# Gated linear attention and a leaky-ReLU block in one kernel: chunks taken in pairs, two tokens per partition

## The chip, the core and the metric

The kernel runs on one core of one Trainium2 chip. The metric is the device time of one execution in microseconds (us), the median of several runs. The profile is one further execution, and its times count from the span's start.

## The reference

Attention with a decaying state, then a two-layer block on its output (batch 4, 8 heads, 768 tokens, head size 48; 3072 tokens of 384 features; hidden size 2048). All inputs are float32.

```python
f = 1 / (1 + exp(-f_logit))
for t in range(768):
    state = f[:, :, t, :, None] * state + outer(k[:, :, t], v[:, :, t])
    y[:, :, t] = q[:, :, t] @ state
x = y.transpose(0, 2, 1, 3).reshape(3072, 384)
h = x @ w_in                      # 384 x 2048
out = maximum(0.01 * h, h) @ w_out  # 2048 x 384
```

## The kernel before

**Units.** A unit is one chunk of 128 tokens of one batch, all heads: 24 units, unit u being chunk u // 4 of batch u % 4, so four neighbouring units are the same chunk of the four batches. Everything that follows attention treats two units (a "pair" m of units 2m and 2m+1) as 256 columns.

**Attention of a unit.** `load_part` loads f, k, q and v on SP's queue, one token per partition: runs of 48 floats, 192 bytes. `gate_exp` and `gate_ln` on ACT give ln(1 + exp(-f)); `gate_pe` sums it over the tokens with a triangular matrix, and with a column of ones gives the chunk's total; `decay_em` and `decay_a` (ACT) are exp of plus and minus that sum, and also the chunk's total decay. `k_scale` and `q_scale` (VectorE or GpSimd) multiply k and q by them and write bf16. `turn_pe` with `turn_k`, `turn_q` (units 4 to 9), or one DMA transpose of two units, `turn2_dma` (units 10 to 23), turn both into kT and qT. `score_pe` multiplies them, `mask` keeps the causal half, `mix_pe` adds the old state's part (qT with `state_b`) and the masked part, `y_out` copies y to bf16, and `x_pe` with `x_out`, or `x2_dma`, turn it into xT. `state_pe`, `state_dve` and `state_pool` carry the state on.

**The block.** For each pair, `up` (eight groups g of 6 matmuls, weights from w_in, 256 columns), `up_act` (ACT, leaky ReLU into gT), then `down` (two halves of 8 matmuls of 384 columns for each unit), `put` into `osb`, and `out_dma`.

**The first four units** (chunk 0 of all batches) run in a special order (functions `q_...`): four tokens per partition, 32 partitions per batch, so runs of 768 bytes, and v is brought into place by the matmuls of `q_pick`. Weights come by GpSimd's queue: `load_w_in` in two halves, `load_w_out` in four quarters.

**Order.** The schedule is manual: after the functions stands a list of some 800 calls, and each engine and queue carries out its own part of it in that order. PE never skips a matmul whose operand is late, and SP's queue holds all loads, turns and stores, one behind the other. All rings (`raws` of 6 units, `kqs` of 4, and so on) are fixed buffers.

Of the kernel before, what the change touches and what calls it, by code (L numbers as in the profile page):

```python
# [15 lines left out]
def kernel(  # L17
# [10 lines left out]
    nc = tc.nc  # L28
# [4 lines left out]
    NCH = S // C  # L33
# [3 lines left out]
    CH = KD // 2  # L37

    units = [(c, b) for c in range(NCH) for b in range(B)]
    NU = len(units)
    NQ = B

    GBUFS = 5
    R_RAW, R_KQS, R_LF, R_EM, R_AEND, R_V, R_KQT, R_WM, R_XN, R_XT = 6, 4, 3, 3, 8, 6, 4, 4, 4, 4
    const = ctx.enter_context(tc.tile_pool(name="const", bufs=1))
    opool = ctx.enter_context(tc.tile_pool(name="opool", bufs=8))
    psum = ctx.enter_context(tc.tile_pool(name="psum", bufs=1, space=bass.MemoryType.PSUM))
    banks = [psum.tile([128, 512], FP32, name=f"ps{i}", tag=f"ps{i}") for i in range(8)]  # L50

    def ring(name, n, shape, dtype):
        return [const.tile(shape, dtype, name=f"{name}{i}", tag=f"{name}{i}") for i in range(n)]

    def bank(i):
        return banks[i][:, :]

    def bank16(i):
        return banks[i][:, :].bitcast(BF16)

    ctx.enter_context(tc.manual_schedule())


    fq = const.tile([128, H, 4, D], FP32, tag="fq")
    kq = const.tile([128, H, 4, D], FP32, tag="kq")
    qq = const.tile([128, H, 4, D], FP32, tag="qq")

    def first_load(eng, name, b, hh=None):
        h = slice(0, H) if hh is None else slice(4 * hh, 4 * hh + 4)
        eng.dma_start(out=fq[32 * b:32 * b + 32, h, :, :].rearrange("p h j d -> p h (j d)"),  # L70
                      in_=f_logit[b, h, 0:C, :].rearrange("h (t j) d -> t h (j d)", j=4))

    def load_all(t, src):
        nc.sync.dma_start(out=t.rearrange("p h j d -> p h (j d)"),  # L74
                          in_=src[:, :, 0:C, :].rearrange("b h (t j) d -> t b h (j d)", j=4))
# [12 lines left out]
    ut = const.tile([128, 128], BF16, tag="ut")
    make_upper_triangular(nc, ut, val=1.0, diag=True)
    us = const.tile([128, 128], BF16, tag="us")  # L90
    make_upper_triangular(nc, us, val=1.0, diag=False)
    ident = const.tile([128, 128], BF16, tag="ident")
    make_identity(nc, ident)
    ones_col = const.tile([128, 1], BF16, tag="ones")
    nc.gpsimd.memset(ones_col, 1.0)

    w_in_b = [const.tile([128, NK, FF // 2], BF16, name=f"w_in{i}", tag=f"w_in{i}") for i in range(2)]
    w_in_p = [t.rearrange("p a (g n i) -> p a g n i", n=128, i=4) for t in w_in_b]
    w_out_b = const.tile([128, NF, KD], BF16, tag="w_out")
# [3 lines left out]
    lfq = [const.tile([128, 4, 4, 64], BF16, name=f"lfq{i}", tag=f"lfq{i}") for i in range(2)]
    khq = [const.tile([128, 4, 4, 64], BF16, name=f"khq{i}", tag=f"khq{i}") for i in range(2)]
    qhq = [const.tile([128, 4, 4, 64], BF16, name=f"qhq{i}", tag=f"qhq{i}") for i in range(2)]
    for t in lfq + khq + qhq:
        nc.vector.memset(t[:, :, :, D:64], 0.0)

    lfs = [const.tile([128, H, 64], BF16, name=f"lf{i}", tag=f"lf{i}") for i in range(R_LF)]
    kqp = ring("kqh", R_KQS // 2, [128, 2, 2, H, 64], BF16)  # L110
    kqs = [kqp[i // 2][:, i % 2] for i in range(R_KQS)]
    khs, qhs = [t[:, 0] for t in kqs], [t[:, 1] for t in kqs]
    state_f = [const.tile([128, P2, D], FP32, name=f"sf{b}", tag=f"sf{b}") for b in range(B)]
    state_b = [const.tile([128, P2, 2 * D], BF16, name=f"sb{b}", tag=f"sb{b}") for b in range(B)]


    block = const.tile([128, 2, 32], BF16, tag="block")
    for b in range(B):
        r = slice(32 * b, 32 * b + 32)
        for i, t in enumerate((ut, us)):  # L120
            nc.vector.tensor_copy(out=block[r, i, :], in_=t[r, r])
    steps = const.tile([128, 4, 32, 4], BF16, tag="steps")
    for i in range(4):
        for t, j0, j1 in ((0, i, 4), (1, 0, i)):
            if j1 > j0:
                nc.vector.tensor_copy(out=steps[:, i, :, j0:j1],
                                      in_=block[:, t, :, None].to_broadcast([128, 32, j1 - j0]))
    for t in lfs:
        nc.vector.memset(t[:, :, D:64], 0.0)
    for t in kqs:  # L130
        nc.vector.memset(t[:, :, :, D:64], 0.0)
    for t in state_b:
        nc.vector.memset(t, 0.0)

# [11 lines left out]


    raws = {name: ring(name, R_RAW, [128, H, D], FP32) for name in ("f_raw", "k_raw", "q_raw", "v_raw")}
    em_ts = ring("em_t", R_EM, [128, H, D], BF16)
    a_ts = ring("a_t", R_EM, [128, H, D], BF16)  # L150
    a_ends = ring("a_end", R_AEND, [128, P2], FP32)
    a_rows = ring("a_row", 2, [128, 2, 64, P2], FP32) if AEND else []
    for t in a_rows:
        nc.gpsimd.memset(t[96:128, :, D:64, :], 1.0)
    v_bs = ring("v_b", R_V, [128, H, D], BF16)
    kqTp = ring("kqT", R_KQT // 2, [128, 2, 2, P2, 128], BF16)
    kqTs = [kqTp[i // 2][:, i % 2] for i in range(R_KQT)]
    turned = {"kT": [t[:, 0] for t in kqTs], "qT": [t[:, 1] for t in kqTs]}
    wms = [ring(f"wm{e}", R_WM, [128, P2, 128], BF16) for e in range(2)]
    xnp = ring("xn", R_XN // 2, [128, 2, KD], BF16)  # L160
    xns = [xnp[i // 2][:, i % 2] for i in range(R_XN)]
    xTs = ring("xT", R_XT, [128, NK, 2, 128], BF16)
    gTs = ring("gT", GBUFS, [128, NF, 2, 128], BF16)
    raw = {}

    def load_part(u, name, src, eng=nc.sync):
        c, b = units[u]
        t = raws[f"{name}_raw"][u % R_RAW]
        eng.dma_start(out=t, in_=src[b, :, c * C:(c + 1) * C, :].rearrange("h t d -> t h d"))  # L169
        raw.setdefault(u, {})[name] = t  # L170

    def load(u):
        for name, src in (("f", f_logit), ("k", k), ("q", q), ("v", v)):
            load_part(u, name, src)

    seen = const.tile([128, 1], FP32, tag="seen")

    def touch(what):
        src = {"f": fq[:, 0, 0, 0:1], "k": kq[:, 0, 0, 0:1], "q": qq[:, 0, 0, 0:1],
               "v": raws["v_raw"][1][:, 0, 0:1], "w": raws["v_raw"][3][:, 0, 0:1]}[what]  # L180
        nc.gpsimd.tensor_copy(out=seen, in_=src)

    def load_w_in(g):
        w = FF // 2
        nc.gpsimd.dma_start(out=w_in_b[g],
                            in_=moe_w_in.rearrange("(a p) n -> p a n", p=128)[:, :, g * w:(g + 1) * w])

    def load_w_out(g):
        w = NF // 4
        nc.gpsimd.dma_start(out=w_out_b[:, g * w:(g + 1) * w, :],  # L190
                            in_=moe_w_out.rearrange("(g p i) n -> p g i n", p=128, i=w)[:, g, :, :])

    st = {u: {} for u in range(NU)}
# [88 lines left out]
    def q_k_mul(hh, pp, bp, bk):  # L282
        q_mul(kTq, emT, hh, pp, bp, bk)
# [1119 lines left out]
```

## Time and profile before

| what | us |
|---|---|
| runs | 182.78, 182.24, 180.99; median 182.24 |
| the profiled execution: its span (no time of its own beside the span is given) | 180.2 |
| PE busy, share of the span | 171.4, 95% |
| ACT, VectorE, GpSimd busy | 124.4, 92.0, 57.9 |
| first matmul of `up` starts | 21.1 |
| units 0 to 3 are mixed, pair 0 and most of pair 1 are up and 20 matmuls of `down` have started | by 34.5 |

The span is the profiler's, from the first to the last instruction; a run is 2.0 us longer than it by the median. PE's busy time counts a matmul from start to its modelled end, and neighbours overlap; a matmul's share of PE's time is therefore read from the distance between starts.

### The profile page before, as it was taken

What the parts mean: (1) busy time and instruction counts of PE and PEld (TensorE: products, weight loads), DVE (VectorE), ACT (ScalarE), POOL (GpSimd) and SP (SyncE); (2) the same over time, 40 slices, a digit from 0 to 9 for tenths busy, and PEclk for the clock granted to TensorE, in tenths of its full rate; (3) what the DMA queues carried; (4) which work ended last, traced back from release to release, by engine and by line L of the source; (5) the groups of instructions that cost most, each with busy time, mean ns of one, the idle gap of its engine ahead of it and who ended that gap; (6) DMA issues with size and microseconds to landing.
All of it is one profiled execution on the core that took longest, in us unless ns stands there. A gap on an engine that the chain in (4) does not pass through costs nothing.

```text
span 180.2 us, 4849 instructions
## 1 busy us (share of the span) xinstructions
PE 171.4 (95%) x1919; PEld 137.8 (76%) x1919; DVE 92.0 (51%) x211; ACT 124.4 (69%) x264; POOL 57.9 (32%) x107
## 2 busy tenths in 40 slices
PE   7689999999999999899999999999999999999992
PEld 5365899677878897597789687789876697798672
DVE  7779860287888735335376186696543266000000
ACT  2779999286887789767488776668795562596331
POOL 7077570023256444700446052634072100000000
PEclk9999999999999999999999999999999999999999
DMA  5999999899997989999699899999999982720112
GB/s 154 312 299 162 197 208 214 156 201 190 155 205 125 215 172 224 165 216 208 147 239 251 181 183 185 209 213 173 203 155 209 224 237 48 60 77 0 44 48 86
DMA packets 109398, 31.31 MB, mean 174 GB/s; under 512 B 100800, under 2 KB 108096, under 8 KB 109376
## 3 DMA queue, kind: packets, MB, share of 16 engines
q1 hardware_dynamic: 107440, 27.47, 79.5%
q0 software_dynamic: 1376, 3.15, 9.5%
q10 hardware_dynamic: 560, 0.39, 0.7%
q8 instruction: 15, 0.25, 0.7%
q14 instruction: 7, 0.06, 0.1%
HBM read 25.17 MB, written 4.72 MB: 166 GB/s over the span
## 4 chain that ended last, share of the span: by engine, by line
PE 58%; SPq 25%; DMA 11%; issue 1%; ACT 1%; DVE 1%; DVEq 0%
SPq L169 24%; PE ps L482 24%; PE ps L502 23%; DMA v_raw<-in_v_dram 6%; DMA f_raw<-in_f_logit_dram 3%; PE ps L420 2%; DMA fq<-in_f_logit_dram 2%; PE ps L441 2%; PE ps L507 1%; PE ps L438 1%; PE ps L348 1%; SPq L74 1%; PE ps L472 1%; PE ps L449 1%; DVE v_b L145 1%
## 5 line engine op out<-in xcount | busy, mean ns | idle before, releaser
L502 PE MATMUL ps<-w_out_b,gT 128*128 128x384 bf16 x368 | 65.9, 326 | 0.0
L487 ACT ACTIVATE gT<-ps 128x512 bf16<-128x512 f32 x88 | 51.5, 602 | 19.1 <-PE ps L482 16.7
L482 PE MATMUL ps<-xT,w_in 128*128 128x256 bf16 x528 | 63.3, 273 | 1.0 <-DVE xT L145 1.0
L482 PEld LDWEIGHTS <-w_in 128*128 128x128 bf16 x528 | 56.4, 114 | 3.0 <-issue 1.2
L502 PEld LDWEIGHTS <-gT 128*128 128x128 bf16 x368 | 34.6, 98 | 19.8
L431 DVE TENSOR_TENSOR wm<-ps,ut 128x512 bf16<-128x512 f32 x40 | 24.9, 683 | 14.5 <-ACT gT L487 4.9
L370 POOL TENSOR_TENSOR kqh<-k_raw,em_t 128x384 bf16<-128x384 f32 x12 | 11.4, 951 | 33.3 <-ACT em_t L355 28.1
L143 ACT COPY osb<-ps 128x384 f32<-128x384 f32 (+1 forms) x22 | 10.2, 465 | 17.0 <-PE ps L502 15.2
L332 POOL CAST sb<-sf 64x192 bf16<-64x192 f32 x40 | 14.5, 363 | 14.9 <-PE ps L438 12.8
L145 DVE CAST v_b<-v_raw 128x384 bf16<-128x384 f32 x14 | 7.1, 505 | 16.0 <-DMA v_raw<-in_v_dram 15.9
L374 DVE TENSOR_TENSOR kqh<-q_raw,a_t 128x384 bf16<-128x384 f32 x13 | 10.0, 770 | 8.0 <-DMA q_raw<-in_q_dram 7.3
L339 ACT ACTIVATE f_raw<-f_raw 128x384 f32<-128x384 f32 x20 | 10.6, 532 | 4.8 <-DMA f_raw<-in_f_logit_dram 4.6
L342 ACT ACTIVATE lf<-f_raw 128x384 bf16<-128x384 f32 x20 | 10.5, 527 | 0.4
L358 ACT ACTIVATE a_t<-ps 128x384 bf16<-128x384 f32 x20 | 9.8, 494 | 1.1 <-PE ps L351 0.9
L145 DVE CAST xn<-ps 128x384 bf16<-128x384 f32 x15 | 8.2, 556 | 4.1 <-PE ps L441 3.4
L355 ACT ACTIVATE em_t<-ps 128x384 bf16<-128x384 f32 x20 | 9.9, 501 | 0.2 <-PE ps L351 0.2
L463 POOL TENSOR_TENSOR sf<-sf,a_end 128x192 f32<-128x192 f32 x16 | 9.5, 592 | 0.4
L145 POOL CAST v_b<-v_raw 128x384 bf16<-128x384 f32 x6 | 3.1, 510 | 19.8 <-DMA v_raw<-in_v_dram 19.8
L137 PE MATMUL ps<-fill 128*128 128x256 bf16 x37 | 7.3, 353 | 1.4 <-DVE fill L102 1.3
L374 POOL TENSOR_TENSOR kqh<-q_raw,a_t 128x384 bf16<-128x384 f32 x7 | 7.0, 1003 | 4.2 <-issue 2.6
L370 DVE TENSOR_TENSOR kqh<-k_raw,em_t 128x384 bf16<-128x384 f32 x8 | 5.9, 752 | 3.7 <-ACT em_t L355 3.7
L441 PE MATMUL ps<-v_b,wm 128*128 128x48 bf16 x160 | 7.2, 183 | 0.0
(89 smaller groups left out, 201.8 us busy)
## 6 DMA issues: line engine op xcount, KB each, us to landing
out_dram<-osb SPq DMA_DIRECT2D x23, 192.0 KB, 3.4
f_raw<-in_f_logit_dram SPq DMA_DIRECT2D x20, 192.0 KB, 4.6
k_raw<-in_k_dram SPq DMA_DIRECT2D x20, 192.0 KB, 4.6
q_raw<-in_q_dram SPq DMA_DIRECT2D x20, 192.0 KB, 4.5
v_raw<-in_v_dram SPq DMA_DIRECT2D x20, 192.0 KB, 4.2
w_in<-in_moe_w_in_dram POOLq DMA_DIRECT2D x2, 768.0 KB, 9.8
w_out_b<-in_moe_w_out_dram POOLq DMA_DIRECT2D x4, 384.0 KB, 8.4
kq<-in_k_dram SPq DMA_DIRECT2D x1, 768.0 KB, 6.6
```

The costliest lines, as they stand in the source:

```text
L145: eng.tensor_copy(out=out, in_=in_)
L169: eng.dma_start(out=t, in_=src[b, :, c * C:(c + 1) * C, :].rearrange("h t d -> t h d"))
L332: nc.gpsimd.tensor_copy(out=state_b[b][r, :, e * D:(e + 1) * D], in_=state_f[b][r])
L339: nc.scalar.activation(raw[u]["f"], raw[u]["f"], AF.Exp, scale=-1.0)
L342: nc.scalar.activation(lfs[u % R_LF][:, :, 0:D], raw[u]["f"], AF.Ln, bias=1.0)
L370: eng.tensor_mul(khs[u % R_KQS][:, :, 0:D], raw[u]["k"], em_ts[u % R_EM])
L374: eng.tensor_mul(qhs[u % R_KQS][:, :, 0:D], r["q"], a_ts[u % R_EM])
L431: nc.vector.tensor_mul(wms[e][u % R_WM], bank(bk).rearrange("p (i n) -> p i n", i=P2), ut[:, None, :].to_broadcast([128, P2, 128]))
L441: nc.tensor.matmul(bank(bk)[:, h * D:(h + 1) * D], wms[h % 2][u % R_WM][:, h // 2, :], v_b[:, h, :], start=False, stop=(h == H - 1))
L482: nc.tensor.matmul(bank(bk)[:, i * 256:(i + 1) * 256].rearrange("p (a n) -> p a n", a=2), w_in_p[ff // 8][:, kk, ff // 4 % 2, :, ff % 4], ...
L487: nc.scalar.activation(gTs[m % GBUFS][:, 2 * g:2 * g + 2].rearrange("p f a n -> p (f a n)"), bank(bk), AF.Prelu, alpha=0.01)
L502: nc.tensor.matmul(bank(bk)[:, 0:KD], g_part(u)[:, ff, :], w_out_b[:, ff, :], start=(ff == 0), stop=(ff == NF - 1))
```

## The change

The kernel is written anew around pairs of another kind, and the list of calls is new too.

- **A pair is now two neighbouring chunks of one batch**: 256 tokens, two per partition (token 2t + j in partition t). Pair m is batch m % 4, chunks 2(m // 4) and 2(m // 4) + 1; partitions 0 to 63 hold the first chunk, 64 to 127 the second. A load takes 256 tokens in runs of 384 bytes: 45 loads of that size (and six of half of it) in place of 80 of 128 tokens. Stores go from 64 partitions, rows of 1536 bytes, two for a pair.
- **Shared gates.** `gate_exp`, `gate_ln`, `decay_em`, `decay_a` work on 768 columns, once for a pair. The two tokens of a partition are added first (`gate_sum`), one `gate_pe` sums a pair, and `gate_base`, `gate_next` (VectorE, GpSimd) give each of the two tokens its own sum.
- **Turns.** `turn_dma` is two DMA transposes of 64 rows, one for each chunk, for pairs 2 to 11; pair 1 is turned on PE. Transposed columns hold even tokens, then odd ones, and the mask is made for that order.
- **v.** `v_cast` makes v bf16 in the two-token layout, which `state_pe` uses (16 matmuls over 64 rows where there were 8 over 128); `v_spread` (four VectorE copies a pair) brings it to one token per partition for `mix`.
- **The first pair** is batch 0's chunks 0 and 1 alone, in halves of four heads (`f_...`); its `up` is done unit by unit (`up1`), and its v is turned by four matmuls (`v_turn`).
- **Weights**: `load_w_in` comes in four quarters, and the calls of both loads stand elsewhere.

Rows of the order on POOL, where the weight loads stand, before (`wm` masks, `sb` states of the first four units):

```order
L181 COPY seen<-qq 128x1
L185 DMA w_in_104<-in_moe_w_in_dram 128x3x1024
L185 DMA w_in_103<-in_moe_w_in_dram 128x3x1024
L145 CAST gT_222<-gT_223 128x768 x2
L300 AFFINE_SELECT wm_213<-wm_213 128x512
L300 AFFINE_SELECT wm_211<-wm_211 128x512
L190 DMA w_out_b<-in_moe_w_out_dram 128x1536
L300 AFFINE_SELECT wm_214<-wm_214 128x512
L190 DMA w_out_b<-in_moe_w_out_dram 128x1536
```

and after (`ls` from `gate_sum`, `rawF` in L257 from `gate_next`, `kh` from `scale`):

```order
L243 TENSOR_TENSOR ls<-rawF 128x8x48
L215 CAST sb<-sf 64x4x48 x2
L127 CAST vq<-rawV 128x768
L227 DMA w_out<-in_moe_w_out_dram 128x1536
L243 TENSOR_TENSOR ls<-rawF 128x8x48
L204 TENSOR_TENSOR sf<-sf,gT 128x192
L257 TENSOR_TENSOR rawF<-rawF 128x8x48 x2
L227 DMA w_out<-in_moe_w_out_dram 128x1536 x2
L272 TENSOR_TENSOR kh<-rawK,em 128x4x2x48 x2
L227 DMA w_out<-in_moe_w_out_dram 128x1536
```

The second and third quarter of w_out now stand behind the gates of pairs 1 and 2, and the fourth behind a scaling.

Rows of the order on SP's queue in the middle of the kernel, before (`kqT` is the turned k and q of two units):

```order
L393 DMA_TRANSPOSE kqT_206<-kqh_124 128x16x128
L169 DMA q_raw_173<-in_q_dram 128x8x48
L169 DMA v_raw_179<-in_v_dram 128x8x48
L169 DMA f_raw_162<-in_f_logit_dram 128x8x48
L169 DMA k_raw_168<-in_k_dram 128x8x48
L393 DMA_TRANSPOSE kqT_205<-kqh_123 128x16x128
```

and after:

```order
L284 DMA_TRANSPOSE kT<-kh 128x16x64 x2
L233 DMA rawQ<-in_q_dram 128x8x96
L233 DMA rawF<-in_f_logit_dram 128x8x96
L233 DMA rawV<-in_v_dram 128x8x96 x2
L233 DMA rawK<-in_k_dram 128x8x96
L284 DMA_TRANSPOSE kT<-kh 128x16x64 x2
```

A pair's turn is two entries of 64 rows, one right behind the other, and the loads between are twice as large.

```diff
-    units = [(c, b) for c in range(NCH) for b in range(B)]
...
-    def load_part(u, name, src, eng=nc.sync):
-        c, b = units[u]
-        t = raws[f"{name}_raw"][u % R_RAW]
-        eng.dma_start(out=t, in_=src[b, :, c * C:(c + 1) * C, :].rearrange("h t d -> t h d"))
+    def load(n, m, s):
+        c = m // 4 * 2 * C
+        nc.sync.dma_start(out=part(n, s).rearrange("p h j d -> p h (j d)"),
+                          in_=SRC[n][m % 4, :, c:c + 2 * C, :].rearrange("h (t j) d -> t h (j d)", j=2))
...
+    def gate_sum(eng, s, l):
+        eng.tensor_add(LS[:, l, :, 0:D], part("F", s)[:, :, 0, :], part("F", s)[:, :, 1, :])
+
+    def gate_pe(l, bk):
+        nc.tensor.matmul(bank(bk)[:, 0:KD], tri, LS[:, l, :, 0:D], start=True, stop=True)
+        for p in range(P2):
+            nc.tensor.matmul(bank(bk)[:, KD + 2 * p:KD + 2 * p + 2], LS[:, l, 2 * p:2 * p + 2, :], ind,
+                             start=True, stop=True)
+
+    def gate_base(s, bk):
+        t = part("F", s)[:, :, 0, :]
+        V.tensor_add(t, bank(bk)[:, 0:KD].rearrange("p (h d) -> p h d", h=H), t)
+
+    def gate_next(eng, s):
+        t = part("F", s)
+        eng.tensor_add(t[:, :, 1, :], t[:, :, 0, :], t[:, :, 1, :])
...
+    def scale(eng, i, s, e, kh):
+        o = KH[:, kh, 1024 * i:1024 * i + 1024].rearrange("p (a j e d) -> p a j e d", a=P2, j=2, e=2)
+        x, y = [t.rearrange("p (a e j d) -> p a e j d", a=P2, e=2, j=2) for t in (RAW["KQ"[i]][:, s], (EM, AA)[i][:, e])]
+        for j in range(2):
+            eng.tensor_mul(o[:, :, j, :, 0:D], x[:, :, j], y[:, :, j])
...
+    def v_spread(t, vb):
+        for w in range(2):
+            for j in range(2):
+                V.tensor_copy(out=VB[64 * j:64 * j + 64, vb, w, :], in_=VQ[64 * w:64 * w + 64, t, j * KD:(j + 1) * KD])
...
-    def turn2_dma(m):
-        nc.sync.dma_start_transpose(out=kqTp[m % (R_KQT // 2)].rearrange("p w i a n -> p (w i a) n"),
-                                    in_=kqp[m % (R_KQS // 2)].rearrange("p w i h d -> p (w i h d)"))
+    def turn_dma(kh, t):
+        for w in range(2):
+            nc.sync.dma_start_transpose(out=KT[:, t, 1024 * w:1024 * w + 1024].rearrange("p (k n) -> p k n", n=64),
+                                        in_=KH[64 * w:64 * w + 64, kh, :])
...
+    def state_pe(kh, t, *bks):
+        for p in range(P2):
+            for j in range(2):
+                for w, bk in enumerate(bks):
+                    r = slice(64 * w, 64 * w + 64)
+                    x = 2 * p + j
+                    nc.tensor.matmul(bank(bk)[:, p * 96:(p + 1) * 96], KH[r, kh, 128 * x:128 * x + 128],
+                                     VQ[r, t, j * KD + p * 96:j * KD + (p + 1) * 96], start=(j == 0), stop=(j == 1))
```

More of the change, by code (lines that the diff above doesn't have):

```diff
@@ L103 @@
[L103 to L110, printed above, removed]
@@ L430, in mask @@
[L430 to L438 removed]
+                nc.tensor.matmul(bank(bks[e])[:, p * 128:(p + 1) * 128], turned(t, w, 0, p)[r], turned(t, w, 1, p)[r],
+                                 start=True, stop=True)
@@ new lines @@
+    state_pe(2, 2, 6, 2)
+    down(0, 3, 4, 1, 0)
+    y_out(A, 1, 0, 1)
+    load('K', 5, 2)
+    x_pe(1, 5)
+    gate_sum(G, 0, 0)
+    state_first(2, 6, 0)
+    x_out(A, 5, 1)
+    put(V, 0, 1, 0)
+    put_state(2, 0)
+    gate_pe(0, 7)
+    put(V, 1, 3, 0)
+    up(0, 0, 1)
+    state_dve(2, 2)
+    up(1, 6, 1)
+    out_pair(0, 1, 0)
+    up_act(0, 0, 1)
+    gate_base(0, 7)
+    state_pool(2, 1, 0)
+    load('Q', 5, 2)
+    score(1, 2, 1, 5)
+    up_act(1, 6, 1)
+    score(0, 2, 3, 2)
+    state_dve(1, 4)
@@ new lines @@
+    turn_dma(2, 2)
+    gate_exp(1)
+    y_out(V, 0, 6, 1)
+    mix(1, 1, (0, 1), [6, 7], 1, 5)
+    gate_ln(1)
+    down(0, 0, 2, 2, 0)
+    v_spread(1, 1)
+    load('Q', 11, 1)
+    y_out(A, 1, 5, 1)
+    decay_a(2, 1)
+    down(0, 1, 2, 2, 0)
+    scale(G, 0, 0, 1, 1)
+    x_dma(1, 3)
+    state_pe(2, 2, 7, 3)
+    put(A, 0, 2, 3)
+    score(1, 2, 4, 1)
+    score(0, 2, 6, 5)
+    down(1, 0, 2, 2, 1)
+    gate_sum(V, 1, 1)
+    scale(G, 1, 2, 1, 0)
+    state_dve(3, 7)
+    down(1, 1, 2, 2, 1)
```

2124 lines of the change are left out of this document (944 added, 1180 removed).

## The prediction

> **What bounds the kernel now.** I read the page's busy times first, then the table by stretches, then PE's rows in order of time, and the chain of waits last.
>
> ```profile
> span 180.2 us, 4849 instructions
> PE 171.4 (95%) x1919; PEld 137.8 (76%) x1919; DVE 92.0 (51%) x211; ACT 124.4 (69%) x264; POOL 57.9 (32%) x107
> ...
> 10.00:20.00 10.00, 9.30 (x149) 6.68 (x147) 8.88 (x23) 9.27 (x24) 5.72 (x9) 1.00 1.13 213
> 20.00:30.00 10.00, 10.00 (x124) 9.76 (x122) 5.55 (x14) 9.12 (x18) 5.72 (x13) 1.00 1.12 208
> 60.00:70.00 10.00, 9.70 (x124) 8.76 (x122) 3.88 (x8) 8.81 (x22) 2.68 (x4) 1.00 0.99 200
> 70.00:80.00 10.00, 8.98 (x95) 7.10 (x93) 4.98 (x12) 7.31 (x20) 5.82 (x10) 1.00 0.97 175
> ...
> PE 58%; SPq 25%; DMA 11%; issue 1%; ACT 1%; DVE 1%; DVEq 0%
> ```
>
> The columns of a stretch are its length, then PE, PEld, DVE, ACT and POOL busy, PE's clock, the DMA engines' share and GB/s. PE is full from 20 us on, at full clock; between 60 and 80 it loses 1.3 us of 20. The DMA engines are full too, and the chain names SP's queue for a quarter of the span; but PE is full beside it, so faster loads are worth the 1.3 us and little more. What counts is how soon PE has work of the block, how much work it has after that, and what it waits for. PE's own prices, from start to start:
>
> ```profile
> 102.60 0.24 PE L351 MATMUL ps<-ones_col,lf 128*128 128x1 bf16 x4
> 102.70 1.46 PE L502 MATMUL ps<-w_out_b,gT 128*128 128x384 bf16 x8
> ...
> 111.17 0.82 PE L482 MATMUL ps<-xT,w_in 128*128 128x256 bf16 x6
> 111.82 0.33 PE L438 MATMUL ps<-sb,kqT 128*128 128x96 bf16 x4
> 111.99 0.36 PE L441 MATMUL ps<-v_b,wm 128*128 128x48 bf16 x8
> 112.20 0.32 PE L348 MATMUL ps<-lf,ut 128*128 128x384 bf16 x1
> 112.36 0.24 PE L351 MATMUL ps<-ones_col,lf 128*128 128x1 bf16 x4
> ...
> 113.28 1.46 PE L502 MATMUL ps<-w_out_b,gT 128*128 128x384 bf16 x8
> 114.57 0.50 PE L472 MATMUL ps<-ident,xn 128*128 128x128 bf16 x6
> 114.91 1.46 PE L502 MATMUL ps<-w_out_b,gT 128*128 128x384 bf16 x8
> ...
> 116.47 0.62 PE L420 MATMUL ps<-kqT 64*128 64x128 bf16 x16
> 117.03 1.48 PE L502 MATMUL ps<-w_out_b,gT 128*128 128x384 bf16 x8
> ```
>
> So a group of `up` costs 0.65 us (0.109 a matmul), half a `down` 1.29 (0.162), `mix` 0.17 + 0.21, a gate 0.16 + 0.10, six transposes 0.34 (0.057 each), 16 score matmuls over 64 rows 0.56 (0.035 each).
>
> **The sum's frame.** I cut the profiled execution at 34.5 us, where its units 0 to 3 are mixed, as the changed kernel's pairs 0 and 1 (also four units) are when `up` of pair 1 begins; that moment I call T1. What PE has left from 34.5 us:
>
> ```profile
> L502 PE MATMUL ps<-w_out_b,gT 128*128 128x384 bf16 x350 | 62.8, 326 | 0.0
> L482 PE MATMUL ps<-xT,w_in 128*128 128x256 bf16 x444 | 53.5, 273 | 1.0 <-DVE xT L145 1.0
> L348 PE MATMUL ps<-lf,ut 128*128 128x384 bf16 x19 | 6.2, 327 | 0.3 <-ACT lf L342 0.3
> L449 PE MATMUL ps<-v_b,kqh 128*128 128x96 bf16 x64 | 5.2, 206 | 0.1
> L472 PE MATMUL ps<-ident,xn 128*128 128x128 bf16 x42 | 4.2, 219 | 0.0
> L383 PE MATMUL ps<-ident,kqh 128*128 128x128 bf16 x48 | 3.7, 219 | 0.0
> ```
>
> Before, 180.2 - 34.5 = 145.7 us remain, waits and tail included. Now the edits, as differences to that.
>
> *The block.* All of it is 24 units of 16 x 0.162 + 24 x 0.109 (two units share a group of 256 columns) = 5.2 us. Before has 84 `up` matmuls and 20 of `down` behind it at the cut, 12.4 us; after has pair 0 behind it at T1, 10.4. So +2.0.
>
> *Shared gates.* Of 19 gates of 0.26 left, nine remain (pair 2's stands before T1): -2.6.
>
> *Turns.* The 48 transposes on PE (L383) go, at 0.057: -2.7. *Turns of x*: 36 instead of 42: -0.3. *States*: 64 matmuls of 96 columns, priced like those of `mix` at 0.17 / 4 = 0.0425, become 112 over 64 rows. They cost at least 0.035 x 96/128 = 0.026, if two halves run side by side as in the scores, at most 0.0425: +0.2 to +2.0. The scores' row is nearest: +0.2. `score` and `mix` keep their counts.
>
> *Loads.* The runs double to 384 bytes and the packets halve. That takes back the 1.3 us of late loads at most: -1.3.
>
> *ACT, VectorE, GpSimd* are hidden as long as PE is the last to be ready. ACT's gates shrink, from one call of 384 columns a unit to one of 768 a pair. GpSimd gets 34 half scalings and 13 additions of 384 elements at 0.95 us in place of 19 scalings, some 27 us more on 58:
>
> ```profile
> L370 POOL TENSOR_TENSOR kqh<-k_raw,em_t 128x384 bf16<-128x384 f32 x12 | 11.4, 951 | 33.3 <-ACT em_t L355 28.1
> L431 DVE TENSOR_TENSOR wm<-ps,ut 128x512 bf16<-128x512 f32 x40 | 24.9, 683 | 14.5 <-ACT gT L487 4.9
> ```
>
> That is about half of the span, no bound in itself; if the cover goes, a scaling that is late holds the turn behind it, then every load behind the turn on SP's queue, then PE.
>
> *Turns by DMA.* This is the new wait. Between the call of `turn_dma` and its `score` the list holds, by the prices above, 4.2, 5.5, 5.0, 5.3, 5.3, 4.8, 3.3, 5.2, 4.0 and 3.9 us of PE's work for pairs 2 to 11. Whole turns of 128 rows took:
>
> ```profile
> L393 SPq DMA_TRANSPOSE kqT<-kqh x7: 1888/3307/4323, 73.7 to 141.7; - x7
> ...
> DMA to landing us min/median/max: 4.3/5.0/6.3
> ...
> 73.68 4.32 SPq L393 DMA_TRANSPOSE kqT<-kqh  x1
> ...
> 138.59 1.89 SPq L393 DMA_TRANSPOSE kqT<-kqh  x1
> ```
>
> The first row is the issue on SP in ns, min, median and max, the second the time to landing; the others are the longest and the shortest issue. No row has a turn of 64 rows. From below, two halves carry a whole turn's bytes and land like the quickest, 4.3: PE waits 0.1 + 1.0 + 0.3 + 0.4 = 1.8 us in all. At the median 5.0 it waits 4.8, at 6.3 it waits 16.5. From above, each half costs a whole one: 3.3 + 5.0 = 8.3, and PE waits some 36. Since the queues carry half the load packets I take 4.3, +1.8.
>
> Sum from T1: 145.7 + 2.0 - 2.6 - 2.7 - 0.3 + 0.2 - 1.3 + 1.8 = 142.8 us.
>
> **T1.** The rows of the head:
>
> ```profile
> kq<-in_k_dram SPq DMA_DIRECT2D x1, 768.0 KB, 6.6
> ...
> fq<-in_f_logit_dram SPq DMA_DIRECT2D x1, 192.0 KB, 3.5
> ...
> 0.81 3.74 DMA fq<-in_f_logit_dram
> ...
> 8.91 1.21 POOL L145 CAST khq<-kq 128x768 bf16<-128x768 f32 x1 [4.72 <-DMA kq<-in_k_dram]
> 10.70 3.45 ACT L250 ACTIVATE gT<-ps 128x256 f32<-128x256 f32 x9 [1.09 <-PE ps L245]
> 11.41 0.58 POOL L181 COPY seen<-qq 128x1 f32<-128x1 f32 x1 [1.29 <-DMA qq<-in_q_dram]
> 13.91 1.60 POOL L145 CAST gT<-gT 128x768 bf16<-128x768 f32 x2 [0.25 <-DMA gT<-in_v_dram]
> 21.10 2.13 PE L482 MATMUL ps<-xT,w_in 128*128 128x256 bf16 x18
> ...
> DMA to landing us min/median/max: 7.0/8.4/10.2
> ```
>
> The last row is w_out's quarters. Before, ACT ends the first units' decays at 10.70 + 3.45 = 14.15. After, f of one pair is two pieces of 192 KB, as large as the one that lands at 4.55; ACT then has 768 columns a step instead of 1536, which I put at half of the 9.6 us that it takes before (4.55 to 14.15): done at 9.4, say 9.6 with twice as many calls. The first `up` moves by that 4.5 us, to 16.6. The loads allow it: k, q and v of 768 KB arrive 2.5 us apart, 314 GB/s, and v of pair 0 ends 1.9 MB instead of 3.1; at 768-byte speed it lands at 10.2, slower with shorter runs, and w_in leaves right after it, where before it left at 11.9.
>
> But pair 0 holds 10.4 us of the block, and then PE needs pair 1 and w_out. GpSimd issues the second and third quarter of w_out only behind both `gate_next`. By estimate f of pair 2 lands at 17.0 (eight loads are the bytes that before had at 13.9, in shorter runs and beside w_in); exp and ln 1.7, `gate_sum` 0.95, gate 0.3, `gate_base` 0.6, two `gate_next` 1.9: 22.5. The quarter then lands at 29.5 to 32.7, by the median 30.9. PE has the scores of pair 1 queued behind the `down` that needs it: two quarters of `down` 1.3, score 0.3, four masks of 0.68, `mix` 0.4, y 0.5, turn 0.3, copy 0.8. So T1 is 35.8 with the quickest landing and 37.2 with the median. Were w_out no brake, k of pair 1 would be scaled by 25.5 and turned and copied by 27.6, and T1 would be 32.6. I take the middle of 32.6 and 37.2, 34.9.
>
> Span 34.9 + 142.8 = 177.7. A run is 2.0 us longer by the median (182.24 against 180.2), so 179.7 us, 1.4% less than the median before.
>
> **Rivals.**
>
> *Same: the head gives nothing and w_out comes late.* T1 is 37.2, the later end: 37.2 + 142.8 + 2.0 = 182.0. For it speaks the landing of 8.4 us in a stretch whose DMA share is 1.12; against it the halved packets of the loads.
>
> *Slower: the turns of 64 rows.* If two halves in a row land after 6.3 us, as the slowest whole turn did, PE waits 16.5 us instead of 1.8 and the run takes 194.4. It decides from some 5.3 us on, where the wait passes the 1.8 by 4.4 and the run passes 184.1. For it speaks that amid the loads, at 73.68, one turn held SP for 4.3 us; against it that in the quiet end, at 138.59, one took 1.9. The Trainium skill (DMA: Bandwidth & Descriptors, Rules for kernel authors) says of two transfers to disjoint partition halves: "Don't bother — they serialize". No run here shows such a pair yet; by that rule this rival's 194.4, not 179.7, is the time to expect.
>
> *Much faster: no wait at all.* T1 32.6, no turn waited for: 32.6 + 142.8 - 1.8 + 2.0 = 175.6; the 145.7 us before hold 138 of work by these prices, so 7.7 of waits and tail, and with half of those gone as well it is 171.8.
>
> **How the numbers follow.** A difference under about 1% (182.24 +- 1.8) can't be told from none. The forecast has 0.45, with a range of its own of 174.0 to 181.5; the case of no wait has 0.07; all but 0.02 of the two is faster by over 1%: faster 0.50. The late w_out has 0.20, and with that 0.02 same is 0.22. The late turns have 0.28: slower 0.28. The whole range reaches up into the late turns, to a landing of about 5.6 us, and down to 173.5: 173.5 to 188.0 leaves out 0.2.
>
> **What will show it.** The start of the first `up` (16.6) and of pair 1's (34.9); w_out's second quarter issued at 22.5 and landed near 30; `gate_pe` 11 times; idle PE in front of the scores in the middle, with DMA as its releaser, 2 us in all for the forecast and over 6 for the slower rival; time to landing of a turn of 64 rows; GpSimd busy near 85 us. I am wrong if PE's gaps after T1 come from GpSimd's scalings or ACT instead, or if 64-row matmuls of the states take 0.04 us or more.

## The result and the profile after

The changed kernel takes 198.43 us (median of 4 runs, 196.19 to 203.29) against 181.76 us before on the same chip, a ratio of 1.0891 with a 95% interval of 1.0794 to 1.0987. The forecast was 179.7 us, and the range ended at 188.0. A second measurement of it, beside later experiments, gave 198.21 us and 1.0979 [1.0896, 1.1062]. Ratios go by undisturbed executions alone (the 203.29 us is a disturbed one), and of the two experiments whose profiled execution was disturbed, the gate behind x and the column halves, only the order of rows is read.

The page of the changed kernel:

```profile
span 196.0 us, 4572 instructions
PE 171.4 (87%) x1829; PEld 134.8 (69%) x1829; DVE 105.5 (54%) x221; ACT 111.2 (57%) x196; POOL 82.0 (42%) x131
...
PE 55%; DMA 29%; DVE 3%; SPq 3%; issue 3%; ACT 2%; POOL 2%; DVEq 0%; POOLq 0%
```

TensorE is busy for the same 171.4 us as before, in a span that is 15.8 us longer; no engine has taken its place as the bound, and the chain of waits names DMA landings for 29%, which it named for 11% before. The table by stretches (length, busy PE, PEld, DVE, ACT, POOL, PE's clock, DMA share, GB/s) shows where TensorE stands still:

```profile
10.00:20.00 10.00, 5.80 (x77) 4.00 (x77) 8.60 (x20) 5.50 (x9) 8.36 (x12) 0.93 1.13 230
20.00:30.00 10.00, 8.06 (x85) 7.81 (x86) 2.32 (x5) 3.58 (x7) 4.77 (x6) 0.55 1.16 235
30.00:40.00 10.00, 9.21 (x126) 6.32 (x124) 7.39 (x15) 4.58 (x8) 4.59 (x9) 1.00 0.97 224
...
40.00:50.00 10.00, 7.53 (x77) 5.97 (x75) 6.22 (x14) 6.48 (x12) 5.20 (x11) 0.83 1.04 215
...
90.00:100.00 10.00, 8.42 (x105) 7.27 (x103) 7.76 (x16) 6.72 (x14) 7.13 (x15) 1.00 1.03 238
...
120.00:130.00 10.00, 8.04 (x86) 5.22 (x85) 6.02 (x13) 3.28 (x5) 6.24 (x9) 1.00 0.88 169
```

The head loses most (4.2 us of 10 at 10 to 20 us, and nearly half the clock in the next stretch); the middle loses up to 2.5 us in ten. TensorE's waits, with total, times and longest:

```profile
PE ps L303 <- DMA kT<-kh: 5.9, 5, 1.6
PE ps L370 <- DMA w_in<-in_moe_w_in_dram: 4.3, 3, 1.8
PE ps L352 <- ACT xn L125: 2.1, 1, 2.1
```

L303 is `score`, L370 `up` of pair 0, L352 the turn of x. The head in order of time, from the timelines of TensorE, SP's queue, GpSimd and ScalarE:

```profile
10.87 5.68 SPq L233 DMA_DIRECT2D rawK<-in_k_dram  x2
...
16.68 6.99 SPq L233 DMA_DIRECT2D rawQ<-in_q_dram  x1
...
17.85 0.86 PE L370 MATMUL ps<-xT,w_in 128*128 128x128 bf16 x12 [1.68 <-DMA w_in<-in_moe_w_in_dram]
...
21.13 1.47 PE L370 MATMUL ps<-xT,w_in 128*128 128x128 bf16 x12 [1.77 <-DMA w_in<-in_moe_w_in_dram]
...
23.81 6.62 PE L370 MATMUL ps<-xT,w_in 128*128 128x128 bf16 x72 [0.81 <-DMA w_in<-in_moe_w_in_dram]
...
28.27 1.80 POOL L272 TENSOR_TENSOR kh<-rawK,em 128x384 bf16<-128x384 f32 x2 [1.50 <-DMA rawK<-in_k_dram]
...
40.22 0.84 ACT L237 ACTIVATE rawF<-rawF 128x768 f32<-128x768 f32 x1 [5.56 <-DMA rawF<-in_f_logit_dram]
...
42.36 0.34 PE L352 MATMUL ps<-ident,xn 128*128 128x128 bf16 x3 [2.11 <-ACT xn L125]
...
43.59 2.63 PE L363 MATMUL ps<-xT,w_in 128*128 128x256 bf16 x12
```

`up` of pair 0 begins at 17.85 us, having waited for the first quarter of w_in, and stops again for the next two; k of pair 1, issued at 10.87, reaches GpSimd at 28.27, more than 17 us later; f of pair 3 holds ScalarE until 40.22, with the y of pair 1 queued behind it. The last row is T1, `up` of pair 1: 43.59 instead of 34.9. From there it is 152.4 us to the end instead of 142.8. The turns of 64 rows, first one pair's two issues on SP and the wait that they end in, then the group's issue times and its landing:

```profile
67.73 5.21 SPq L284 DMA_TRANSPOSE kT<-kh  x2
...
74.77 0.62 PE L303 MATMUL ps<-kT 64*128 64x128 bf16 x16 [0.90 <-DMA kT<-kh]
```

```profile
L284 SPq DMA_TRANSPOSE kT<-kh x20: 1246/1852/4110, 39.1 to 143.9; - x20
...
DMA to landing us min/median/max: 3.5/4.1/6.2
```

One half lands 4.1 us after its issue, but it is the second that ends the wait: 7.0 us after the first was issued. In the chain of waits the second lands at 64.6, 74.7, 88.2, 95.4 and 126.1 us, 7.0, 7.0, 7.9, 7.4 and 5.6 us after its pair's first issue.

### The profile page after: what moved, and what is told of

The parts are those of the page before. It is cut to its first block, busy times and chain, and to the rows that moved or that the text cites. A ratio compares the mean times of both kernels' runs of the same rounds, so it can differ in the third digit from the quotient of the medians.

```text
span 196.0 us, 4572 instructions
## 1 busy us (share of the span) xinstructions
PE 171.4 (87%) x1829; PEld 134.8 (69%) x1829; DVE 105.5 (54%) x221; ACT 111.2 (57%) x196; POOL 82.0 (42%) x131
## 2 busy tenths in 40 slices
DMA packets 80132, 33.06 MB, mean 169 GB/s; under 512 B 74864, under 2 KB 79600, under 8 KB 80112
## 3 DMA queue, kind: packets, MB, share of 16 engines
q1 hardware_dynamic: 77408, 29.43, 67.7%
## 4 chain that ended last, share of the span: by engine, by line
PE 55%; DMA 29%; DVE 3%; SPq 3%; issue 3%; ACT 2%; POOL 2%; DVEq 0%; POOLq 0%
PE ps L363 25%; PE ps L383 20%; DMA kT<-kh 11%; DMA w_in<-in_moe_w_in_dram 6%; DMA rawV<-in_v_dram 5%; DMA xT<-xn 4%; DMA rawF<-in_f_logit_dram 4%; PE ps L370 3%; PE ps L303 2%; PE ps L388 1%; PE ps L316 1%; SPq L87 1%; DVE wm L308 1%; PE ps L246 1%; PE ps L313 1%
## 5 line engine op out<-in xcount | busy, mean ns | idle before, releaser
L383 PE MATMUL ps<-w_out,gT 128*128 128x384 bf16 x368 | 64.8, 326 | 0.0
L383 PEld LDWEIGHTS <-gT 128*128 128x128 bf16 x368 | 34.5, 98 | 20.9
L308 DVE TENSOR_TENSOR wm<-ps,mask 128x512 bf16<-128x512 f32 (+1 forms) x50 | 31.0, 663 | 9.9 <-PE ps L303 9.5
L272 POOL TENSOR_TENSOR kh<-rawK,em 128x384 bf16<-128x384 f32 x20 | 18.6, 952 | 12.2 <-ACT em L263 8.6
L280 DVE COPY vb<-vq 64x384 bf16<-64x384 bf16 x44 | 18.3, 416 | 2.5 <-PE ps L316 1.2
L335 POOL TENSOR_TENSOR sf<-sf,aend 128x192 f32<-128x192 f32 x15 | 8.4, 560 | 16.6 <-DVE sf L332 16.4
L303 PE MATMUL ps<-kT 64*128 64x128 bf16 x192 | 9.2, 218 | 6.5 <-DMA kT<-kh 5.9
L237 ACT ACTIVATE rawF<-rawF 128x768 f32<-128x768 f32 x11 | 9.3, 842 | 9.0 <-DMA rawF<-in_f_logit_dram 9.0
L332 DVE TENSOR_TENSOR sf<-sf,ps 64x192 f32<-64x192 f32 x32 | 11.2, 350 | 5.4 <-POOL sb L215 2.0
L272 POOL TENSOR_TENSOR kh<-rawQ,aa 128x384 bf16<-128x384 f32 x14 | 13.1, 957 | 1.2 <-ACT aa L266 1.1
L303 PEld LDWEIGHTS <-kT 64*128 64x128 bf16 x192 | 5.8, 94 | 10.0 <-DMA kT<-kh 7.1
L370 PE MATMUL ps<-xT,w_in 128*128 128x128 bf16 x96 | 8.9, 278 | 4.3 <-DMA w_in<-in_moe_w_in_dram 4.3
L370 PEld LDWEIGHTS <-w_in 128*128 128x128 bf16 x96 | 8.4, 136 | 4.7 <-DMA w_in<-in_moe_w_in_dram 4.7
L263 ACT ACTIVATE em<-rawF 128x768 bf16<-128x768 f32 x11 | 9.3, 843 | 1.3 <-DVE rawF L257 1.1
## 6 DMA issues: line engine op xcount, KB each, us to landing
w_in<-in_moe_w_in_dram POOLq DMA_DIRECT2D x4, 384.0 KB, 10.5
```

What stands on the lines that cost most here:

```text
L237: A.activation(RAW["F"][:, s], RAW["F"][:, s], AF.Exp, scale=-1.0)
L272: eng.tensor_mul(o[:, :, j, :, 0:D], x[:, :, j], y[:, :, j])
L280: V.tensor_copy(out=VB[64 * j:64 * j + 64, vb, w, :], in_=VQ[64 * w:64 * w + 64, t, j * KD:(j + 1) * KD])
L303: nc.tensor.matmul(bank(bks[e])[:, p * 128:(p + 1) * 128], turned(t, w, 0, p)[r], turned(t, w, 1, p)[r], start=True, stop=True)
L308: V.tensor_mul(WM[:, wm, c].rearrange("p (i n) -> p i n", n=128), bank(bk)[:, c].rearrange("p (i n) -> p i n", n=128), masks(4 if hh is No ...
L332: V.tensor_add(SF[r, b], SF[r, b], pt[r, :, e * D:(e + 1) * D])
```

## The experiments

Ratios are to the kernel before on the same chip, with 95% intervals; "T1" is read from TensorE's timeline.

**The head: w_in earlier.** The four `load_w_in` move up to behind `f_cast(G, 1, 1, 0, 0)`, and `touch('V')`, which made them wait for v of pair 0, goes.

> The changed kernel with one edit: GpSimd issues the four quarters of w_in right after its last cast of q, some 2 us earlier, without waiting for v of pair 0; the loads on SP's queue keep their order. Theory 1 (the head is bound by the bytes of all its loads together, and k of pair 1, which landed at 28.2 us, counts as much as w_in): the three waits for w_in shrink from 4.3 us to under 2, k of pair 1 lands no earlier, pair 1's first up stays within 1.5 us of 43.6 and the run within 1% of the changed kernel's 198.4. Theory 2 (w_in alone holds the head): pair 1's up begins by 40 and the run is 194 to 195.

1.0981 [1.0908, 1.1054], T1 44.8: nothing gained, though w_in is waited for 0.5 us only. ScalarE's and TensorE's rows:

```profile
24.81 0.84 ACT L237 ACTIVATE rawF<-rawF 128x768 f32<-128x768 f32 x1 [10.46 <-DMA rawF<-in_f_logit_dram]
...
27.65 0.48 PE L246 MATMUL ps<-ls,tri 128*128 128x384 bf16 x1 [9.32 <-POOL ls L243]
```

What w_in gains, f of pair 2, issued at 8.6 us behind it, loses: it lands 16.2 us after its issue, and pair 2's gate, which stands in TensorE's order between the quarters of `up`, now waits 9.3 us.

**The head: loads in order of due time.** The order on SP's queue, before and after the edit (the letter is the input, the number the pair):

```
-K0 Q0 Q1 V0 F1 V1 F2 Q2 K1 K2 Q3 V2 K3 F3 K4
+K0 Q0 V0 F1 K1 F2 Q1 V1 K2 V2 F3 Q2 K3 Q3 K4
```

> The changed kernel with its head's loads in order of due time on SP's queue: v, f, k of pairs 0 and 1, f of pair 2, q and v of pair 1 first; k, v, q of pair 2 and all of pairs 3 and 4 behind w_in and the first quarter of w_out. Nothing else moves. Theory 1 (order of bytes in the head): with 3.5 MB + 1.6 MB of w_in ahead at some 250 GB/s the last quarter of w_in is there by 20.5 us instead of 23.8, k of pair 1 lands near 18 instead of 28.2, pair 1's up begins at 37 to 40 instead of 43.6, and the run is 192 to 195. Theory 2 (weights' landing is GpSimd's own and the loads don't matter): w_in's waits stay at 4.3 us and the run at 198. Theory 3 (the middle eats the head's gain): pair 1's up comes 4 to 6 us earlier, the waits for kT grow by as much from 5.9, and the run stays above 196.

1.0991 [1.0911, 1.1072]. v of pair 1 is now the load behind w_in, lands 14.7 us after its issue, and pair 2's gate stands behind its cast on GpSimd: the same gap of TensorE, 6.1 us. So GpSimd's cast and VectorE's spread of that v were moved behind pair 1's first scaling and turn as well:

> As the run with the head's loads in order of due time, and on GpSimd the cast of v of pair 1 behind the first scaling of k, on VectorE the spreading of pair 1's v behind its turn's copy, so that f of pair 2 no longer stands behind v of pair 1 (which landed at 24.3 us there, 14.7 us after its issue). Theory 1 (the head is an order of bytes and of queues): the six-microsecond wait before the gates of pair 2 goes, pair 1's up begins at 36 to 39 instead of 43.3, and the run is 191 to 194. Theory 3 (the middle eats it): pair 1's up is as early, but waits before the scores and for VectorE and GpSimd grow, and the run stays above 195. Theory 2' (the weights' 3.1 MB and not the order set it): pair 1's up stays above 41.

1.0912 [1.0857, 1.0967], T1 still 43.6: the gap before the gate is gone, and TensorE waits 3.26 us, until 38.99, for GpSimd, which stood behind q of pair 2, now late in the order. Three orders, one end: whichever load goes late, something that stands before T1 waits for it.

**The head: clock and gate.** 29 `idle_pe` matmuls in front of the waits for w_in:

> The changed kernel with 29 more matmuls on zeros (256 columns, as its idle_pe has them) on TensorE in front of the three places where up waits for w_in; nothing else. Theory 1 (k of pair 1 holds what comes behind): the clock stays near 1.00 in 20 to 30 us, up's 72 matmuls take about 4.2 us instead of 6.6, yet the turn of pair 1 still waits for k scaled at 30.1, so that pair 1's up moves by less than 1 us and the run by less than 0.5%. Theory 4 (the halved clock itself costs the time): 2.6 us less until pair 1's up, 1 us less behind it, run near 195.

1.0987 [1.0893, 1.1081]. The clock is 1.00 in 20 to 30 us and the 72 matmuls take 4.21 us instead of 6.62, yet T1 is 43.02 (43.05 in the second measurement of the changed kernel): the halved clock cost nothing here. Next pair 3's gate behind pair 1's x:

```
-gate_exp(0)  gate_ln(0)  gate_sum(G, 0, 0)  gate_pe(0, 7)  gate_base(0, 7)
 x_out(A, 5, 1)
+gate_exp(0)  gate_ln(0)  gate_sum(G, 0, 0)
 ...
 up(2, 0, 1)
+gate_pe(0, 7)  gate_base(0, 7)
```

> The changed kernel with pair 3's gate (exponential and logarithm on ScalarE, its sum on GpSimd) behind pair 1's turned x, and its matmuls and base behind the third group of up. Theory 8 (f of pair 3, 5.6 us late on ScalarE, holds y and x of pair 1 queued behind it): the 2.1 us wait for xn and the slower clock behind it go, pair 1's up begins at 40 to 41, and the run falls by 2 to 3.5 us, a ratio of 1.08 to 1.085. Rival (the wait moves to pair 3's own gate, turn and scores, whose work starts 2 us later): pair 1's up begins as early, the ratio stays above 1.09.

1.0863 [1.0767, 1.0959], not to be told from the changed kernel. TensorE's rows:

```profile
41.94 1.47 PE L363 MATMUL ps<-xT,w_in 128*128 128x256 bf16 x12 [0.89 <-ACT xT L125]
47.31 0.75 PE L303 MATMUL ps<-kT 64*128 64x128 bf16 x16 [3.90 <-DMA kT<-kh]
```

`up` begins earlier, and the same time is lost one step on, before pair 2's scores.

**The head: fewer bytes.** Pair 2 works on pair 1's k, q, v.

> The changed kernel without the loads of k, q and v of pair 2; pair 2 uses pair 1's k, q and v in their place (so what is computed for pair 2 is not the reference's). Everything else is issued as before, with 1.18 MB less for the DMA engines in front of pair 1's up. Theory 2' (the volume in front of pair 1's up sets it, at the 235 GB/s that the head shows): 1.18 MB are 5 us; pair 1's up begins at 37.5 to 40 instead of 43, and the run is 193 to 195, a ratio of 1.07 to 1.08. Rival (the order on the engines sets it, not the loads): pair 1's up stays above 41.5 and the ratio above 1.09.

1.0973 [1.0928, 1.1017], but this run tells nothing: in my edit the load of pair 4's k came ahead of pair 2's scaling and became its source. VectorE's row shows it:

```profile
36.90 1.03 DVE L272 TENSOR_TENSOR kh<-rawK,em 128x384 bf16<-128x384 f32 x2 [7.01 <-DMA rawK<-in_k_dram]
```

Mended:

```
-load('K', 2, 2)  load('Q', 2, 2)  load('V', 2, 2)  load('K', 4, 1)
-scale(V, 0, 2, 1, 2)  scale(G, 1, 2, 0, 2)  v_cast(G, 2, 2)
+scale(V, 0, 1, 1, 2)  scale(G, 1, 1, 0, 2)  load('K', 4, 1)  v_cast(G, 1, 2)
```

> As the run with less to load, mended: there the load of pair 4's k stood in the program ahead of pair 2's scaling and so became its source, and VectorE waited 7 us for it. Now it stands behind. Pair 2 uses pair 1's k, q and v (its result is not the reference's), and 1.18 MB less are loaded ahead of pair 1's up. Theory 2' (the volume ahead of pair 1's up, 5 us at 235 GB/s): pair 1's up begins at 38 to 40 instead of 43, the run is 193.5 to 195.5, a ratio of 1.07 to 1.08. Rival (the order of work on the engines): above 41.5 and above 1.09.

1.0621 [1.0520, 1.0722], 192.57 us. T1 by the row of `up`:

```profile
39.19 1.47 PE L363 MATMUL ps<-xT,w_in 128*128 128x256 bf16 x12
```

That is 4 us earlier, and the run keeps it (151.7 us follow, where 152.4 and 153.0 did). No reordering did that; 1.18 MB less did. The edit takes away the waits for these loads too, but the load that held T1 last in the changed kernel is another, f of pair 3, and it is still there. ScalarE's row shows it 4.4 us earlier, as T1 is:

```profile
35.82 0.84 ACT L237 ACTIVATE rawF<-rawF 128x768 f32<-128x768 f32 x1 [2.72 <-DMA rawF<-in_f_logit_dram]
```

**The turns: no one waits for them.** The scores and mixes of pairs 2 to 11 read slot 1.

> The changed kernel with all its transposes by DMA issued as they are, into slots that nobody reads (one slot more); the scores and the mixes of pairs 2 to 11 read pair 1's transposed k and q instead, so what is computed for these pairs is not the reference's. Theory 5 (the pairs of 64-row turns are late, and that is what the middle loses): the 5.9 us of waits before the scores go, pair 1's up stays at 43.6, and the run falls by 5 to 7 us to some 192. Theory 6 (they only stand in for other waits behind them): other waits (x turned by DMA, states on GpSimd, late loads) take their place and the run falls by less than 3 us.

1.0776 [1.0707, 1.0845], by the ratios 3.7 us less than the changed kernel, give or take 1.9. The waits for kT are gone; others are in their place:

```profile
PE ps L367 <- DVE sf L336: 2.3, 2, 1.5
PE ps L317 <- POOL sb L216: 2.0, 2, 1.8
```

**The turns left out** (the same reads, `turn_dma` issues nothing):

> As the run in which nobody reads the turned k and q of pairs 2 to 11, but with the 20 transposes by DMA left out altogether (what is computed for these pairs is not the reference's). Theory 6 (waits behind the turns take over): the run is within 1% of that run's ratio, 1.078. Theory 7 (the turns cost by holding SP, 3 to 5 us a pair, and with it all loads and stores behind them): another 3 us or more less than that, a ratio of 1.06 or lower.

1.0523 [1.0476, 1.0569], 189.65 us: by the ratios the turns cost another 4.6 us by being there, not by being waited for. By queue shares times span, the packets of SP's queue (q1) fall from 67.7% of 196.0 to 51.5% of 187.9 us, from 133 to 97 us of all sixteen DMA engines.

**The turns: one of 128 rows.**

```
-for w in range(2): dma_start_transpose(out=KT[:, t, 1024*w:1024*w+1024]... n=64, in_=KH[64*w:64*w+64, kh, :])
+dma_start_transpose(out=KT[:, t]... n=128, in_=KH[:, kh, :])
```

> The changed kernel with one transpose by DMA of 128 rows and 2048 columns for each pair in place of two of 64 rows; it writes the same bytes of the same slot, but the columns stand in another order, so what is computed for pairs 2 to 11 is not the reference's. Theory 5 (two halves in a row cost two full turns): from issue to landing falls from the pair's 7 to 8 us to 5 to 6, the waits before the scores fall under 3 us and the ratio by 0.01 to 0.02. Rival (the bytes set it, not the number of instructions): the issue takes 4 us or more, landing 7 to 8 us, and the waits stay at 6.

1.0579 [1.0530, 1.0629], 190.84 us, where the changed kernel had 198.21 beside it. T1 is 42.65; what follows takes 146.3 instead of 153.0 us. The waits for kT, and the whole turns with their landing:

```profile
PE ps L301 <- DMA kT<-kh: 0.4, 1, 0.4
```

```profile
L283 SPq DMA_TRANSPOSE kT<-kh x10: 1935/3426/4861, 38.0 to 135.3; - x10
...
DMA to landing us min/median/max: 4.3/5.4/7.1
```

The same bytes land 5.4 us after the issue in the median (4.3 to 7.1), where a pair of halves needed 6.8 (5.6 to 7.9). Is it the second instruction or the 64 rows? Two halves again, but by columns, k then q, 128 rows each:

> Two transposes by DMA for each pair as in the changed kernel, but of 128 rows and 1024 columns each (k, then q) in place of 64 rows and 2048 columns; same bytes. The columns stand in another order, so what is computed for pairs 2 to 11 is not the reference's. Theory 9 (the second instruction costs: another of the eight transfers that SP can have under way, and another landing): the pair needs 6.5 to 8 us from issue to landing, and the ratio is 1.085 to 1.10 as with 64 rows. Rival (64 rows are the dear thing): landing and ratio as with one transpose of 128 rows, 1.055 to 1.065.

1.0576 [1.0524, 1.0627], 190.57 us: as good as one whole turn. Theory 9, the price of a second instruction, falls by this ratio; the 64 rows are dear. The three forms by themselves, behind the end of the changed kernel, each set held back by a copy on VectorE:

> The changed kernel with turns alone behind its end, on empty queues, each set held back by a copy of the one before: four times two turns of 64 rows and 2048 columns, four times two of 128 rows and 1024 columns, four times one of 128 rows and 2048 columns, 512 KB each set. The run is longer by these sets; only their rows count. If 64 rows are dear in themselves: a pair of 64-row turns needs 1 us or more longer from the first issue to the last landing than a pair of column halves (in the quiet end of earlier runs 5.6 to 5.9 against 4.9 to 5.2 us), and the single one lies within 0.5 us of the column halves. If they are dear only beside loads: all three within 0.3 us.

VectorE's wait for one set of each form, from its copy before to the set's last landing (but for the very first, the sets of a form differ by at most 0.14 us):

```profile
205.56 0.69 DVE L1193 COPY kh<-kT 128x2048 bf16<-128x2048 bf16 x1 [5.64 <-DMA kT<-kh]
...
228.70 0.69 DVE L1197 COPY kh<-kT 128x2048 bf16<-128x2048 bf16 x1 [4.58 <-DMA kT<-kh]
...
249.29 0.69 DVE L1200 COPY kh<-kT 128x2048 bf16<-128x2048 bf16 x1 [4.36 <-DMA kT<-kh]
```

Two of 64 rows take 5.6 us, two by columns 4.6, one whole 4.4, on empty queues: 64 rows are dear in themselves, and not only beside loads. The Trainium skill (DMA: Bandwidth & Descriptors, Rules for kernel authors) says that two transfers to disjoint partition halves serialize and should be one. The trace agrees that halves gain nothing; that halves by columns cost 0.2 us and halves by rows 1.3 is what these rows add.

**The turns on two queues.** `(nc.sync, nc.scalar)[w].dma_start_transpose(...)`:

> The changed kernel with the second 64-row turn of every pair issued from ScalarE's queue, the first still from SP's. Theory 7 (SP held by two issues in a row): SP is held 1.3 to 2.7 us a pair instead of 3.2 to 5.4, the pair lands 5 to 6 us after its issue instead of 7 to 8, and the run falls by 4 to 7 us, a ratio of 1.06 to 1.075. Rival (the two halves share what they wait for, or ScalarE held by the issue holds TensorE's banks): ScalarE is held 1.3 us or more for each of ten turns, the landing stays at 7 to 8 us, and the ratio stays above 1.085.

1.1918 [1.1849, 1.1986], 215.43 us, on the rival's side and far beyond it. One pair's turns on the two queues:

```profile
67.66 1.26 ACTq L284 DMA_TRANSPOSE kT<-kh  x1
...
73.83 1.24 SPq L284 DMA_TRANSPOSE kT<-kh  x1
```

SP's turn starts 6.2 us after ScalarE's (3.8 to 6.2 for the four pairs between 56 and 97 us), 0.1 us after that one has landed, though SP had nothing else to issue: just before, the trace has SP waiting for the semaphore that ScalarE's turn raises, so that the program itself sets one half behind the other. The same rules of the Trainium skill ask for just this, that a turn on one queue wait until those of the other have completed; what two turns under way at once would do, no run here shows. TensorE then waits 13.7 us for kT.

**Whole turns that compute the reference.** In the runs with a whole turn and with column halves, the columns of kT stand in an order that its readers do not expect. Here the readers split by token parity: `score` as 32 matmuls of 64 x 64, the state's part of `mix` as 8 of 128 x 64.

> The changed kernel with one 128-row turn for each pair, and what reads it written for that order of columns: from pair 1 on a score is 32 matmuls over 64 rows into 64 partitions instead of 16 into 128, the part of mix that reads the state 8 matmuls into 64 partitions instead of 4 into 128. It computes all of the reference. If 64 rows by 64 partitions run four at a time, scores cost the same 0.56 us and the ratio is that of the whole turn, 1.055 to 1.065. If they run only two at a time as now, 20 scores cost 0.56 us more each and 20 mixes 0.17 to 0.34 us: 14 to 18 us more of TensorE, a ratio of 1.13 to 1.16.

1.0838 [1.0773, 1.0904], 194.84 us: between the two cases. 32 scores take no longer than 16, and the eight state matmuls 0.29 us (66.49 to 66.78) where four took 0.17:

```profile
61.90 0.64 PE L310 MATMUL ps<-kT 64*64 64x128 bf16 x32
...
66.49 0.36 PE L325 MATMUL ps<-sb,kT 128*64 128x96 bf16 x8
66.78 0.37 PE L328 MATMUL ps<-vb,wm 128*128 128x48 bf16 x8
```

19 mixes with a state cost 2.3 us by that; the rest of the 4.7 us by which this kernel is slower than the whole turn alone is not shown. It computes all of the reference some 3 us faster than the changed kernel (the two intervals just touch), and is still 8% slower than the one before.

**Together.** First three edits at once, the whole turn, the gate behind x and the spoilt one:

> Three edits together: one 128-row turn for each pair (7.4 us less by itself), no loads of k, q, v of pair 2, and pair 3's gate behind pair 1's turned x. What is computed for pairs 2 to 11 is not the reference's. If these three are what the changed kernel loses against the kernel before, and do not overlap: pair 1's up begins at 36 to 38, what follows takes 146 us, and the run is 183.5 to 186, a ratio of 1.02 to 1.035. If the head's gains are lost behind pair 1's up: 188 or more, above 1.045.

1.0885 [1.0829, 1.0942]: VectorE waits for pair 4's k again, and TensorE stands still for 5.1 us amid the scores of pair 1, so nothing follows. Then the whole turn with the mended edit:

> One 128-row turn for each pair, and no loads of k, q, v of pair 2 (what is computed is not the reference's from pair 2 on). If volume ahead of pair 1's up and turns are separate costs, they add: 190.8 - 4 = 186 to 188, a ratio of 1.03 to 1.043. If the head's gain is lost behind pair 1's up, 190 or more, a ratio above 1.053.

1.0422 [1.0363, 1.0482], 187.30 us. T1 is 39.29, the rest 145.9 us, as long as the 145.7 us after the cut before; what is still lost against the kernel before lies in the head. By ratios to the second measurement of the changed kernel the two edits give 0.040 and 0.036, together 0.056: they overlap by a quarter, though each has an interval of some 0.01 about it. With the fills on top:

> One 128-row turn for each pair, no loads of k, q, v of pair 2, and the 29 matmuls on zeros in front of the waits for w_in (what is computed is not the reference's from pair 2 on). Theory 4 (the slower clock in 20 to 30 us costs once the loads no longer hide it): 1 to 2 us less than without the fills, a ratio of 1.03 to 1.037 against 1.042. Theory 1 (k of pair 1 and w_out hold what follows all the same): no less, 1.04 or more.

1.0366 [1.0295, 1.0438], 187.40 us; intervals that overlap, T1 39.58: the clock's share can't be told from nothing here either.

## Why the prediction was wrong

*TensorE's own work was priced rightly.* After T1 it is busy for 139.7 us. Before, 141.1 were left at the cut; with +2.0, -2.6, -2.7, -0.3 and +0.2 that makes 137.7, and 1.3 us of the rest is `up` at half clock (12 matmuls in 2.63 us at 43.59). 64-row matmuls of the states ran at 0.028 us (16 in 0.44), `gate_pe` 11 times, GpSimd 82.0 us.

*T1 failed, by 8.7 us.* The step that failed is "the loads allow it", and with it the whole estimate of what stands before T1. w_in did leave right after v of pair 0, at 9.83 us; what came late was its landing, and that of the loads beside and behind it. I followed each load by itself, at the landing times of before, and did not add up the bytes. From 10 to 40 us the sixteen engines are full at 224 to 235 GB/s (217 to 265 with the other orders); until T1 they moved 43.6 us x 230 GB/s = 10.0 MB, against 34.5 x 216 = 7.5 MB at the cut before. Of this 1.2 MB are k, q and v of pair 2, whose scaling, cast and states stand before pair 1's `up` on each engine. The six loads that SP issued from 9.7 to 28.3 us landed 10.5 to 20.0 us after their issue. The single steps: first `up` 17.85, not 16.6; the second quarter of w_out issued at 25.6, not 22.5, since `gate_pe` stands behind `up`'s wait for w_in; k of pair 1 scaled by 30.1, not 25.5; then v of pair 2 and f of pair 3. The quarter of w_out, on which I spent the estimate, was waited for 0 us. Taking out the 1.2 MB gives 4.4 of the 8.7 us back. What holds T1 at 39.2 to 39.6 then is not shown; w_in is still waited for 3.6 to 4.4 us, but filling these waits moved nothing, and from 22.9 us on TensorE is busy for 15.4 of the 16.3 us that are left until 39.2.

*The turns failed, by 4.1 us of waits and more behind them.* The step is "two halves carry a whole turn's bytes and land like the quickest, 4.3". A pair needs 5.6 to 7.9 us. The rival named this mechanism, but its arithmetic was wrong too: 6.3 us were to cost 16.5, and 7 us cost 5.9, because SP reaches a turn before TensorE reaches the place in the list from which I counted (67.73 against 68.55 us for pair 4), so the cover was more in fact: 6.1 us for pair 4, where I had 5.0. And waits are not the whole price: by the ratios the run wins 3.7 us without them, 8.2 without the turns, 7.2 with whole turns. So whole turns are not to be told from none by these intervals, and it is the 64 rows that this kernel pays for. How turns that nobody waits for cost 4.6 us is shown only as far as that the ten pairs hold SP for 41.1 us in all (3.2 to 5.5 a pair) and take the engines 36 us, where whole turns hold SP for 34.0 and take 32; which load or store was late for it is not shown.

*Smaller terms.* With the -1.3 for late loads hardly a wait but that for kT was left (0.1 us). In fact after T1 TensorE waits 1.4 us for x turned by DMA and some 1.2 for VectorE's and GpSimd's sums, states and masks. The end after the last matmul is 4.2 us, not 3.2: the last two stores hold SP 0.6 us each, 0.33 before. With 4.1 for kT, 1.3 for the clock, 2.6 and 1.0 this makes 9.0 of the 9.6 us.

## What to carry to other kernels

Where the DMA engines are full, add up the bytes that stand, on any engine's order, before the point of interest and divide by the measured rate; three orders of the same loads did not beat that sum here, and a halved clock in that stretch was free. Price a pair of transfers from the first issue to the last landing, in the loaded stretch. And try a DMA transpose with all 128 rows first: where a split is wanted, a split by columns cost next to nothing here, and one by rows 7 us.

## What the runs showed of the hardware

Two DMA transposes of 64 x 2048 keep VectorE waiting for 5.6 us when they run alone, two of 128 x 1024 for 4.6 and one of 128 x 2048 for 4.4, for the same 512 KB; in the kernel that is 198.2 against 190.6 and 190.8 us. Alone, a half of 64 rows lands 3.9 us after its issue, a half of 128 rows 3.2 (medians). 32 score matmuls of 64 x 64 took 0.64 us where 16 of 64 x 128 take 0.62. With fewer, longer runs the rate of the head's loads rose by about a tenth only: packets fell from 109,398 to 80,132, and from 10 to 30 us the engines moved 230 and 235 GB/s, where they had moved 213 and 208.
